# A complex recurrence and a mixture of experts on one core: less zero fill, a first slice in halves, spaced index casts, one more expert finished by rows

## Chip, cores and metric

The kernel runs on one core of one Trainium2 chip. The metric is the device time of one execution in microseconds. A measurement of this kernel can tell a difference of about 0.2% (1.3 us) from none.

## What is computed

The attention stage is a complex diagonal recurrence over 768 steps for 4 batches and 8 heads of 48 dimensions. Its output, 3072 rows of 384, goes through a router with one choice per row, eight experts of two layers (384 to 1024 to 384) and a capacity of 768 rows:

```python
mag = np.sqrt(a_re**2 + a_im**2)
scale = np.minimum(mag, 0.999) / (mag + 1e-06)
for t in range(S):
    S_re, S_im = ar*S_re - ai*S_im + outer(k[t], v[t]), ar*S_im + ai*S_re
    y[:, :, t] = np.einsum('bhd,bhde->bhe', q[:, :, t], S_re)
...
expert_idx = np.argmax(x @ w_gate, axis=1)
disp[e, counts[e]] = x[i]
h = np.maximum(disp @ w1, 0); y = h @ w2
out[i] = gate_w[i] * y[expert_idx[i], pos[i]]
```

## The kernel before, in words

**Attention.** The sequence is cut into 8 chunks of 96 positions, two chunks to a group `g` (0 to 3). For each group the decays are normalised in six slices of 8 rows (`norm`, L278: load of tile `a`, a square on ACT at L305, a sum of two squares, which PE does by identity matmuls into tile `n` at L272, then logarithm, exponent and corrections on ACT and DVE up to L374). `scan` multiplies the decays step by step on DVE (`xy` at L404, `a` at L409), `post` turns the products into weighted queries and keys (`qko`), which POOL writes to a DRAM scratch `scr`; SP reads them back as `qkc`. A `unit` (batch and chunk, 32 of them) transposes them (`tr`, L629), forms a masked product (`pa` L645, `a_sb` L649 on DVE), the state (`s_all` L660) and the output `y` (L706, L711), and writes the next chunk's state `z`, which POOL finishes by two accumulating DMAs (`z<-sx`, L673).

**Routing.** After the last unit of a cut (`CUTS`, pairs of group and unit count) `routing` picks the expert of each row: logits `lg` (L952) and counts `pp` (L970 to L975) on PE, choice, slot and place on DVE, then for each unit an index cast on DVE (`idx`, L1010) and an indirect DMA on POOL (`disp<-x,idx`, L1024) that scatters 96 rows into the experts' buffer `disp`, 448 rows of 386 words for each expert. Each such scatter is called a send below. `Plan.op(...).apart` keeps two sends apart in the plan, by `APART[b]` us.

**Fill.** Slots that no row reaches have to read as zero with an index out of bounds. Seven DMAs of 512 rows each, 772 KB (`disp<-fill`, L853), write all 3584 rows ahead of the first send.

**Experts.** `Moe.run` goes through 8 places of 8 steps. Place 0 is expert 0, the others are ordered by their counts, with 428 down to 372 rows (`WIDTH`). A step is 9 matmuls of the first layer (`ph`, L1220), ReLU split in two on ACT and DVE (`hh`, `hl`), and 9 of the second layer two steps later (`my`). Places 0 to 6 build the output with features on partitions (`second`, L1228), copy it to `ys` and turn it by PE (`yt`, L1174) before the scaling (`o`, L1184) and the scatter to the output. The last place has rows on partitions (`second_rows`, L1241) and needs neither copy nor turn.

**Order.** The order of attention and routing on every engine comes from `Plan.solve`: each step has an engine, a duration, a due time (`want`) and predecessors; a list scheduler fills the engines and the order is written out. On the chip every engine runs its list in that order and waits on semaphores alone; nothing holds a step back until its planned time. `BEGIN` holds the due times of the groups. `fill_gaps` puts warming matmuls of a 128x128 identity (`keep`, L226, in tile `s_all`) into planned idle time of PE of over 0.4 us that lies behind 82 us of the plan:

```python
if end > begin and gap > least:
    k = int((gap - .15) / one)
    out.append(Op("PE", 0, lambda k=k: keep(k), ...))
```

Of the kernel before, what the change touches and what calls it, by code (L numbers as in the profile page):

```python
# [180 lines left out]
class Att:  # L181
# [96 lines left out]
    def norm(self, g, j, s0):  # L278

# [27 lines left out]
        if g == 0 and j < 1:  # L307
            def xb():
                x = self.a4[g, j][:, 0:n, 3, :]
                nc.vector.tensor_tensor(out=x, in0=st['sq'][:, 0], in1=st['sq'][:, 1], op=ALU.add)  # L310
                st[0] = x
            o = plan.op(None, "DVE", dve(n * D), xb, w, after=[o], bufs=[a4_])
            parts = [(0, n, o, a4_)]
        elif by_dma:
# [66 lines left out]
    def scan(self, g, j, wants):  # L381
# [4 lines left out]
        a4_ = ("a4", g, j)  # L386
        for s in range(n - 1, -1, -1):
# [25 lines left out]
            m = plan.op(None, "DVE", .27, None, want, after=before + [K + ("i",), K + ("r",)], bufs=bufs)  # L413
# [316 lines left out]
    def routing(self, b, c, w, span):  # L730
# [55 lines left out]
CUTS = [(0, 8), (1, 8), (2, 8), (3, 5), (3, 6), (3, 7), (3, 8)]  # L786
# [4 lines left out]
class Route:  # L791
# [54 lines left out]
    def clear_ops(self):  # L846
# [190 lines left out]
class Moe:  # L1037
# [119 lines left out]
    def finish_ops(self, e, tail, py):  # L1157
# [35 lines left out]
    def run(self, order, perm, check):  # L1193
# [89 lines left out]
        for t in range(len(LAST)):  # L1283
# [150 lines left out]
def uncovered(nc, const, ps, sums, smalls, route, out):  # L1434


    bad = const.tile([128, NG + 2], F32, name="bad")
# [14 lines left out]
    nc.vector.tensor_reduce(out=bad[:C, NG + 1:NG + 2], in_=route.over, op=ALU.max, axis=AX.X)  # L1452
    one = const.tile([128, 1], F32, name="one")
# [12 lines left out]
def kernel(ctx, tc, q, k, v, a_re, a_im, w_gate, w1, w2, av, xv, cen, vp, out):  # L1466
# [5 lines left out]
    with ExitStack() as c_main, ExitStack() as c_att:  # L1472
# [143 lines left out]
```

## Time and profile before

| | |
|---|---|
| three runs | 640.61, 640.82, 641.45 us; median 640.82 |
| profiled execution, own time | 641.58 us |
| its span, first to last instruction | 639.9 us |
| mean granted TensorE clock | 0.936 of full |
| busy: PE, DVE, ACT, POOL | 561.8, 458.9, 383.5, 212.9 us |
| moved by DMA | 108.81 MB |

Times in the rows are microseconds from the start of the span. The kernel has two halves: attention and routing to 399 us, then the experts. Shares of the span are means over both; every statement below is read from one stage. A line number is that of the kernel before.

### The profile page before, as it was taken

Reading aid. Unit: us, or ns where it says so; the run is one execution under the profiler, and the core shown is the slowest. Engines: PE = TensorE matmul, PEld = TensorE weight load, DVE = VectorE, ACT = ScalarE, POOL = GpSimd, SP = SyncE. Lnnn points to the kernel's source line nnn. Section 1 sums busy time; section 2 is a strip of 40 time slices with the busy share of each in tenths; the row PEclk is TensorE's granted clock in tenths of the full one; section 3 lists DMA queues with packets and bytes.
Section 4 is the critical chain, followed back from the end, with each engine's and each line's share of the span. In section 5 each row is a group of like instructions: output and inputs, shape, how many; then the busy total and the mean of one; then the engine's idle time right before and its main releaser. Section 6 shows DMA issues by size and latency. Waiting matters only on the chain.

```text
span 639.9 us, 13273 instructions
## 1 busy us (share of the span) xinstructions
PE 561.8 (88%) x4662; PEld 489.7 (77%) x4662; DVE 458.9 (72%) x1340; ACT 383.5 (60%) x1034; POOL 212.9 (33%) x293
## 2 busy tenths in 40 slices
PE   2364569998999989999896889999999999999994
PEld 1122258786887868888785877999999999999993
DVE  3899979999999998999763244546665655655651
ACT  6465689989998899977652421344445344444540
POOL 9532314524459925464525031002020202112012
PEclk9666679999999999999999779999999999999997
DMA  6985588968899787885997231364545454455311
GB/s 214 297 245 147 147 203 231 241 189 207 196 230 251 213 228 168 213 223 135 215 242 209 55 91 29 109 184 125 163 129 158 138 169 155 155 165 159 101 37 37
DMA packets 75629, 108.81 MB, mean 170 GB/s; under 512 B 11716, under 2 KB 65853, under 8 KB 75553
## 3 DMA queue, kind: packets, MB, share of 16 engines
q1 hardware_dynamic: 58192, 57.37, 33.3%
q0 software_dynamic: 17360, 50.50, 29.1%
q8 instruction: 39, 0.64, 0.4%
q14 instruction: 38, 0.30, 0.2%
HBM read 71.51 MB, written 32.47 MB: 163 GB/s over the span
## 4 chain that ended last, share of the span: by engine, by line
PE 55%; DVE 20%; DMA 10%; ACT 9%; issue 4%; POOL 1%; POOLq 0%; DVEq 0%; ACTq 0%; SPq 0%
PE ph L1220 17%; PE my L1228 15%; DVE xy L404 4%; DMA scr<-qko 3%; DVE a L409 3%; PE pa L645 3%; PE tr L629 2%; DMA raw<-in_moe_w_dram 2%; PE n L272 2%; PE my L1241 2%; DMA qkc<-scr 2%; DVE qko L452 2%; PE s_all L660 2%; PE y L706 2%; DMA a<-in_av_dram 2%
## 5 line engine op out<-in xcount | busy, mean ns | idle before, releaser
L1266 ACT ACTIVATE hh<-ph 128x448 fp32r<-128x448 f32 (+7 forms) x64 | 32.7, 511 | 92.1 <-PE ph L1220 81.8
L1267 DVE SCALAR_TENSOR_TENSOR hl<-ph,hh 128x448 fp32r<-128x448 f32 (+7 forms) x64 | 37.2, 581 | 60.4 <-ACT hh L1266 59.6
L1185 POOL DMA_INDIRECT out_dram<-o,xr x26 | 25.7, 987 | 162.8 <-DVE o L1184 159.5
L1130 DVE TENSOR_TENSOR lo<-raw,hi 128x384 fp32r<-128x384 f32 (+2 forms) x128 | 65.7, 553 | 9.8 <-ACT hi L1129 9.7
L272 PE MATMUL n<-a,ident 128*128 128x384 f32 x92 | 44.8, 622 | 28.7 <-ACT a L305 28.7
L1220 PE MATMUL ph<-xh,hi 128*128 128x448 f32 (+7 forms) x192 | 69.5, 362 | 0.0
L1220 PE MATMUL ph<-xh,lo 128*128 128x448 f32 (+7 forms) x192 | 66.5, 347 | 0.0
L404 DVE TENSOR_TENSOR xy<-a 128x192 f32<-128x192 f32 (+1 forms) x199 | 61.5, 322 | 1.3 <-ACT a L374 1.1
L1129 ACT CAST hi<-raw 128x384 fp32r<-128x384 f32 (+2 forms) x128 | 59.1, 512 | 2.8 <-DMA raw<-in_moe_w_dram 2.8
L673 POOL DMA_DIRECT2D z<-sx x56 | 47.4, 1003 | 39.8 <-PE pa L645 12.4
L629 PE MATMUL tr<-ident,qkc 81*96 81x81 f32 x512 | 53.8, 241 | 5.6 <-DMA qkc<-scr 2.6
L1228 PE MATMUL my<-hh,lo 128*128 128x448 f32 (+6 forms) x168 | 58.7, 349 | 0.0
L1228 PE MATMUL my<-hh,hi 128*128 128x448 f32 (+6 forms) x168 | 58.6, 349 | 0.0
L1228 PE MATMUL my<-hl,hi 128*128 128x448 f32 (+6 forms) x168 | 58.6, 349 | 0.0
L649 DVE TENSOR_TENSOR a_sb<-pa,mask 96x384 f32<-96x384 f32 x64 | 35.1, 552 | 32.1 <-PE pa L645 21.1
L1024 POOL DMA_INDIRECT disp<-x,idx x32 | 42.1, 1315 | 46.1 <-DVE lm L961 22.4
L645 PE MATMUL pa<-qT,kT 128*96 128x96 f32 x512 | 56.9, 256 | 0.5 <-issue 0.4
L629 PEld LDWEIGHTS tr<-ident,qkc 81*96 81x96 f32 x512 | 43.3, 130 | 13.3 <-issue 4.0
L645 PEld LDWEIGHTS pa<-qT,kT 128*96 128x96 f32 x512 | 51.2, 170 | 2.5 <-issue 1.6
L272 PEld LDWEIGHTS n<-a,ident 128*128 128x128 f32 x92 | 20.0, 237 | 42.8 <-ACT a L305 24.6
L272 PE MATMUL p<-qko,ident 128*128 128x384 f32 x80 | 37.4, 598 | 15.3 <-ACT qko L441 15.2
L409 DVE TENSOR_TENSOR a<-xy 128x96 f32<-128x96 f32 (+1 forms) x218 | 49.8, 240 | 0.4
(224 smaller groups left out, 1459.0 us busy)
## 6 DMA issues: line engine op xcount, KB each, us to landing
raw<-in_moe_w_dram SPq DMA_DIRECT2D x64, 384.0 KB
qkc<-scr SPq DMA_DIRECT2D x32, 480.0 KB
scr<-qko POOLq DMA_DIRECT2D x44, 192.0 KB
scr<-qko POOLq DMA_DIRECT2D x20, 384.0 KB
a<-in_av_dram POOLq DMA_DIRECT2D x18, 384.0 KB
qkin<-in_xv_dram POOLq DMA_DIRECT2D x18, 384.0 KB
disp<-fill POOLq DMA_DIRECT2D x7, 772.0 KB
v<-in_vp_dram SPq DMA_DIRECT2D x32, 144.0 KB
```

The costliest lines, as they stand in the source:

```text
L272: nc.tensor.matmul(out=pt[:, :m], lhsT=self.ident, rhs=t[:, h:h + m], start=i == 0, stop=i == 1)
L404: nc.vector.tensor_tensor(out=st['xy'][:, :, cs].rearrange("p (u z) d -> p u z d", u=2), in0=a4[:, s, :, cs].rearrange("p (u z) d -> p u z ...
L409: nc.vector.tensor_tensor(out=self.a4[g, j][:, s, 0:2, cs], in0=xy[:, 0:4:2, cs], in1=xy[:, 1:4:2, cs], op=ALU.add)
L629: nc.tensor.transpose(out=pt[:, h * C:h * C + NE], in_=qk[:NE, 4 * hh + h, z_ * C:z_ * C + C], identity=self.ident[:NE, :NE])
L645: nc.tensor.matmul(out=pa[:, h * C:h * C + C], lhsT=kT[:, 4 * hh + h], rhs=qT[:, 4 * hh + h], start=True, stop=True)
L673: nc.gpsimd.dma_start(out=zn[a.start:a.stop or C], in_=st['sx'][o], accum_op=ALU.add)
L1024: ins = nc.gpsimd.indirect_dma_start(out=self.disp, out_offset=bass.IndirectOffsetOnAxis(ap=idx[:, c:c + 1], axis=0), in_=self.row(b, c0 + ...
L1129: return (lambda: nc.scalar.copy(out=hi[i][:, s], in_=raw[i][:, s]), lambda: nc.vector.tensor_tensor(out=lo[i][:, s], in0=raw[i][:, s], in ...
L1130: lambda: nc.vector.tensor_tensor(out=lo[i][:, s], in0=raw[i][:, s], in1=hi[i][:, s].bitcast(F32), op=ALU.subtract))
L1220: nc.tensor.matmul(out=ph[:, :W], lhsT=a[:, k, fs], rhs=r[:, k, :W], start=i == 0, stop=i == len(parts) - 1)
L1228: nc.tensor.matmul(out=py[m][:, :W], lhsT=a[:, f % self.PF, ms], rhs=r[:, :W], start=f == 0 and i == 0, stop=f == NF - 1 and i == 2)
L1267: nc.vector.scalar_tensor_tensor(out=hl[:, :W], in0=ph[:, :W], scalar=0.0, in1=hh[:, :W].bitcast(F32), op0=ALU.max, op1=ALU.subtract)
```

## The change

1. **Fill.** Place 0 is still filled whole (448 rows). Of the seven others only rows 320 to 447 are filled. `uncovered` adds a test: a smallest count under 320 sets the flag that sends the whole computation to the general path at the end. The fills are due at 9 and at 43 to 49 us of the plan, instead of 9, 12, 15 ... 27.
2. **First slice.** Slice (0, 0) goes through `norm_first` in two halves of four rows, the later rows first; the sum of squares stays on DVE. The scan of a row waits for its half alone. All five numbers of `BEGIN` are 3 lower.
3. **Casts.** `apart` is set on the cast (DVE), not on the send (POOL), with 5, 5, 2 and 1.4 us for the groups instead of 5, 5, 2.6 and 1. A new cut (3, 4) routes the first four units of the last group by themselves.
4. **Warming.** `fill_gaps` works from 58 us of the plan on instead of 82.
5. **Seventh place.** Places of three row tiles (`BY_ROWS`: places 6 and 7) use `second_rows`; place 6 loses its copies to `ys` and its turns.

```diff
     def norm(self, g, j, s0):
+        if g == 0 and j == 0:
+            self.norm_first(s0)
+        else:
+            self.norm_slice(g, j, s0)
+    def norm_first(self, s0):
...
+        for p, h in enumerate(range(n - HALF, -1, -HALF)):
+            i = slice(h, h + HALF)
...
+            o = plan.op(K + ("load", p), "SP", .6, load, v - 14, bufs=[a_], kb=48 * HALF, extra=2.)
+            o = plan.op(K + ("xa", p), "ACT", act(2 * m) + .1, xa, v, after=[o], bufs=[a_, a4_])
+            x_ = plan.op(None, "DVE", dve(m), xb, v, after=[o], bufs=[a4_])
...
+        def ready(s):
+            p = ((n - 1 - s) // HALF,) if g == 0 and j == 0 else ()
+            return [K + ("i",) + p, K + ("r",) + p]
...
             x = plan.op(None, "DVE", .12, fs['cast'][i], w + (5 + i) * s, after=[o])
-            o_ = plan.op(K(("send", i)), "POOL", 1.0, fs['send'][i], ...)
+            plan.op(K(("send", i)), "POOL", 1.0, fs['send'][i], ...)
             if rt.scattered is not None:
-                o_.apart = (rt.scattered, APART[b])
-            rt.scattered = o_
+                x.apart = (rt.scattered, APART[b])
+            rt.scattered = x
-BEGIN = (13, 67, 135, 203, 271)
+FILL = (9, 43, 44, 45, 46, 47, 48, 49)
+LEAST = 320
+HALF = 4
+BEGIN = (10, 64, 132, 200, 268)
-APART = (5, 5, 2.6, 1)
+APART = (5, 5, 2, 1.4)
-CUTS = [(0, 8), (1, 8), (2, 8), (3, 5), (3, 6), (3, 7), (3, 8)]
+BY_ROWS = [e for e, w in enumerate(WIDTH) if len(tiles(w)[1]) == KT]
+CUTS = [(0, 8), (1, 8), (2, 8), (3, 4), (3, 5), (3, 6), (3, 7), (3, 8)]
-        dv = self.disp.rearrange("(r p a) x -> r p a x", p=128, a=4)
-        return [lambda r=r: nc.gpsimd.dma_start(out=dv[r], in_=fill.unsqueeze(1).broadcast_to([128, 4, XW]))
-            for r in range(E_ * self.T // 512)]
+        dv = self.disp.rearrange("(e s) x -> e s x", e=E_)
+        def zero(e, s):
+            n = self.T - s
+            a = n // 16 if n < 256 else 4
+            p = n // a
+            nc.gpsimd.dma_start(out=dv[e, s:].rearrange("(p a) x -> p a x", a=a),
+                                in_=fill[:p].unsqueeze(1).broadcast_to([p, a, XW]))
+        return [lambda: zero(0, 0)] + [lambda e=e: zero(e, LEAST) for e in range(1, E_)]
-            pt = py[t] if e == E_ - 1 else turn(t)
+            pt = py[t] if e in BY_ROWS else turn(t)
-                if x[0] < E_ - 1:
-                    second(*x)
+                if x[0] in BY_ROWS:
+                    fin = self.finish_ops(x[0], rows[x[0]]['tail'], x[4]) if x[1] == NF - 1 else None
+                    for t in range(KT):
+                        second_rows(*x, t)
+                        if fin:
+                            fin[1 + t]()
+    nc.vector.tensor_scalar(out=bad[:C, NG + 2:NG + 3], in0=route.rank[:, E_ - 1:], scalar1=float(LEAST - T), scalar2=None, op0=ALU.is_lt)
-        plan.fill_gaps(att.keep)
+        plan.fill_gaps(att.keep, begin=58.)
```

How the order moves, at three places. First POOL near the start, where constants end and the first stores of `scr` begin. Before, with the last two of seven fills there:

```order
L874 TENSOR_TENSOR key<-key,dec 96x8
L877 MEMSET room 96x1 x8
L853 DMA disp<-fill 512x1x386 x2
L498 DMA scr_1_97<-qko_0_327 64x8x96
L495 DMA scr_1_97<-qko_0_327 64x1536
L498 DMA scr_1_97<-qko_0_327 64x8x96
L498 DMA scr_1_97<-qko_1_391 64x8x96
L293 DMA a_0_460<-in_av_dram 128x2x384
```

and now:

```order
L972 TENSOR_TENSOR key<-key,dec 96x8
L975 MEMSET room 96x1 x8
L586 DMA scr_1_97<-qko_0_331 64x8x96
L583 DMA scr_1_97<-qko_0_331 64x1536
L586 DMA scr_1_97<-qko_0_331 64x8x96
L586 DMA scr_1_97<-qko_1_404 64x8x96
L384 DMA a_0_469<-in_av_dram 128x2x384
L583 DMA scr_1_97<-qko_1_404 64x1536
L586 DMA scr_1_97<-qko_1_404 64x8x96
L950 DMA disp<-fill 128x1x386 x2
L586 DMA scr_1_97<-qko_2_471 64x8x96
L950 DMA disp<-fill 128x1x386
```

One fill of 448 rows stays ahead of this piece; the seven small ones stand between the stores of slices 1 to 3 of group 0.

Second, PE from the start to the end of group 0 (`n` are sums of a slice's decays, `ptok` the token numbers that a mask on DVE needs, `pt` and `te` the turns at the group's end). Before, the rows up to `ptok` and those around `pt`:

```order
L272 MATMUL n_1_0_174<-a_0_1_168,ident 128x384 x2
L272 MATMUL n_2_0_190<-a_0_2_182,ident 128x384 x2
L272 MATMUL n_3_0_254<-a_0_3_248,ident 128x384 x2
L240 MATMUL ptok<-ident,tokrow 96x96
```

```order
L272 MATMUL n_1_0_607<-a_1_1_599,ident 128x384 x2
L272 MATMUL p_4_0_624<-qko_4_605,ident 128x384 x2
L563 MATMUL pt_684<-ident,pend_678 96x128 x2
L272 MATMUL n_2_0_708<-a_1_2_696,ident 128x384 x2
L521 MATMUL te_1_0_716<-ident,qko_5_673 96x128 x4
L521 MATMUL te_1_4_727<-ident,qko_5_673 96x128 x4
```

and now:

```order
L272 MATMUL n_1_0_190<-a_0_1_180,ident 128x384 x2
L272 MATMUL n_2_0_218<-a_0_2_204,ident 128x384 x2
L240 MATMUL ptok<-ident,tokrow 96x96
L272 MATMUL p_0_0_339<-qko_0_331,ident 128x384 x2
L272 MATMUL n_3_0_354<-a_0_3_336,ident 128x384 x2
```

```order
L272 MATMUL p_4_0_622<-qko_4_616,ident 128x384 x2
L272 MATMUL n_1_0_646<-a_1_1_626,ident 128x384 x2
L226 MATMUL s_all<-ident 128x128 x18
L272 MATMUL n_2_0_723<-a_1_2_698,ident 128x384 x2
L651 MATMUL pt_740<-ident,pend_695 96x128 x2
L609 MATMUL te_1_0_744<-ident,qko_5_690 96x128 x4
```

`ptok` no longer stands behind the sum of slice 3, and 18 warming matmuls stand ahead of the sum of slice 2 of group 1, itself now ahead of `pt`.

Third, DVE at the end of the routing of group 2 (`a_sb` are the masked products of the next units). Before, eight casts in two bunches:

```order
L1006 TENSOR_REDUCE fine<-ok_0_4836 96x1
L1010 CAST idx_0_4844<-slot_0_4803 96x1 x3
L649 TENSOR_TENSOR a_sb_123<-pa_6_0_4815,mask 96x384
L649 TENSOR_TENSOR a_sb_123<-pa_6_1_4852,mask 96x384
L1010 CAST idx_0_4844<-slot_0_4803 96x1 x5
L649 TENSOR_TENSOR a_sb_122<-pa_7_0_4920,mask 96x384
```

and now, the first five of eight:

```order
L1104 TENSOR_REDUCE fine<-ok_0_4891 96x1
L1108 CAST idx_0_4899<-slot_0_4858 96x1
L737 TENSOR_TENSOR a_sb_123<-pa_6_0_4870,mask 96x384
L737 TENSOR_TENSOR a_sb_123<-pa_6_1_4907,mask 96x384
L1108 CAST idx_0_4899<-slot_0_4858 96x1 x2
L737 TENSOR_TENSOR a_sb_122<-pa_7_0_4968,mask 96x384
L1108 CAST idx_0_4899<-slot_0_4858 96x1
L737 TENSOR_TENSOR a_sb_122<-pa_7_1_4994,mask 96x384
L1058 TENSOR_REDUCE mx_0_5036<-lg_0_5016 96x4
L1059 TENSOR_TENSOR lm_0_5037<-lg_0_5016,mx_0_5036 96x32
```

The casts now alternate with masked products that wait for PE, and with the choice of the new cut.

## Rows read from the trace of the kernel before

**Rows 1.** The page, part 2: PE's granted clock in 40 slices.

```profile
PEclk9666679999999999999999779999999999999997
```

**Rows 2.** Busy time by stretch: PE, PEld, DVE, ACT, POOL, clock, DMA share, GB/s.

```profile
30.00:40.00 10.00, 5.49 (x8) 2.52 (x8) 10.00 (x35) 5.06 (x10) 2.68 (x4) 0.54 1.03 336
...
100.00:120.00 20.00, 19.84 (x211) 15.73 (x210) 20.00 (x55) 19.39 (x63) 11.18 (x16) 1.00 0.93 234
...
400.00:640.00 240.00, 230.69 (x1310) 224.27 (x1309) 133.06 (x283) 99.11 (x219) 29.43 (x30) 0.99 0.44 132
```

**Rows 3.** The chain that ended last, first 20 us: start, duration, what.

```profile
0.82 3.81 DMA a<-in_av_dram
...
12.01 6.04 DMA a<-in_av_dram
```

**Rows 4.** Timeline, DVE, first 25 us: start, duration, engine, line; idle before and releaser.

```profile
13.04 0.43 DVE L404 TENSOR_TENSOR xy<-a 128x96 f32<-128x96 f32 x2 [1.12 <-ACT a L374]
...
13.63 0.55 DVE L344 TENSOR_TENSOR lnn<-n,lnn 128x384 f32<-128x384 f32 x1
...
14.10 0.35 DVE L404 TENSOR_TENSOR xy<-a 128x192 f32<-128x192 f32 x1
...
22.38 0.25 DVE L242 TENSOR_TENSOR mask<-ptok,tokrow 96x96 f32<-96x96 f32 x1 [2.33 <-ACT tokcol L241]
```

**Rows 5.** The same chain: sums of slices near the end of group 0, and one later.

```profile
74.45 2.93 PE n L272 x4
...
85.62 2.93 PE n L272 x4
...
127.64 1.35 PE n L272 x4
```

**Rows 6.** Busy time by stretch, columns of rows 2, group 0 into group 1.

```profile
86.00:90.00 4.00, 4.00 (x13) 2.50 (x13) 3.90 (x15) 2.13 (x6) 1.42 (x2) 0.50 1.08 244
```

**Rows 7.** Timeline, POOL, first and last send of two bursts.

```profile
342.19 1.04 POOL L1024 DMA_INDIRECT disp<-x,idx  x1 [0.30 <-DVE a_sb L649]
...
350.93 0.92 POOL L1024 DMA_INDIRECT disp<-x,idx  x1 [0.30 <-issue]
370.44 0.93 POOL L1024 DMA_INDIRECT disp<-x,idx  x1 [18.58 <-DVE lm L961]
...
375.38 0.92 POOL L1024 DMA_INDIRECT disp<-x,idx  x1 [0.30 <-ACT qT L633]
```

**Rows 8.** Timeline, PE and ACT, stops inside the bursts.

```profile
352.12 0.55 PE L924 MATMUL y<-xt,wg 128*32 128x96 f32 x8 [5.37 <-issue]
...
374.76 0.26 PE L711 MATMUL y<-qT,z 128*48 128x96 f32 x1 [0.49 <-issue]
...
377.65 0.29 PE L629 MATMUL tr<-ident,qkc 81*96 81x81 f32 x1 [1.14 <-issue]
...
351.58 0.48 ACT L900 COPY xt<-y 128x384 f32<-128x384 f32 x1 [8.34 <-remote]
```

**Rows 9.** Busy time by stretch, columns of rows 2, behind the stops.

```profile
352.00:360.00 8.00, 6.39 (x60) 5.82 (x60) 1.11 (x2) 2.78 (x9) 0.00 (x0) 0.50 0.36 89
...
377.60:384.00 6.40, 6.35 (x47) 5.64 (x48) 1.81 (x7) 1.69 (x5) 0.37 (x1) 0.51 0.41 111
```

**Rows 10.** A lone send of group 1, and the stretch that holds four such.

```profile
264.28 1.01 POOL L1024 DMA_INDIRECT disp<-x,idx  x1 [3.20 <-DVE idx L1010]
...
260.00:280.00 20.00, 19.87 (x236) 16.77 (x236) 19.73 (x69) 17.64 (x53) 9.98 (x13) 1.00 0.77 196
```

**Rows 11.** Timeline, PE: eleven warming matmuls, two passes each.

```profile
386.67 2.70 PE L226 MATMUL s_all<-ident 128*128 128x128 f32 x22
```

**Rows 12.** Timeline, PE: six of place 6's turns, and the matmul behind them.

```profile
610.78 0.82 PE L1174 MATMUL yt<-ident,ys 128*128 128x128 f32 x6
611.36 0.42 PE L1220 MATMUL ph<-xh,hi 128*128 128x372 f32 x1
```

**Rows 13.** Timeline, POOL: the longest send of group 0.

```profile
205.72 5.92 POOL L1024 DMA_INDIRECT disp<-x,idx  x1 [0.30 <-issue]
```

More of the change, by code (lines that the diff above doesn't have):

```diff
@@ L280, in norm, with norm_slice @@
+    def norm_slice(self, g, j, s0):
         nc, plan = self.nc, self.plan
@@ L306, in norm @@
         o = plan.op(K + ("xa",), "ACT", act(2 * n * D) + .1, xa, w, after=[K + ("load",)], bufs=[a_, a4_])
[L307 to L314, printed above, removed]
+        if by_dma:
             def acc():
@@ L412, in scan @@
             before = [("s", g) + prev[1:]] if ("s", g) + prev[1:] in plan.names else []
-            m = plan.op(None, "DVE", .27, None, want, after=before + [K + ("i",), K + ("r",)], bufs=bufs)
+            m = plan.op(None, "DVE", .27, None, want, after=before + ready(s), bufs=bufs)
             a = plan.op(("s", g, j, s), "DVE", .169, None, want, after=[m], bufs=[a4_, xy_])
@@ L750, in routing @@
             x = plan.op(None, "DVE", .12, fs['cast'][i], w + (5 + i) * s, after=[o])
-            o_ = plan.op(K(("send", i)), "POOL", 1.0, fs['send'][i], w + (5 + i) * s, after=[x] + ([("mload",)] if (b, c + 1) in LATE else []), kb=148, extra=2.)
+            plan.op(K(("send", i)), "POOL", 1.0, fs['send'][i], w + (5 + i) * s, after=[x] + ([("mload",)] if (b, c + 1) in LATE else []), kb=148, extra=2.)
             if rt.scattered is not None:
-                o_.apart = (rt.scattered, APART[b])
-            rt.scattered = o_
+                x.apart = (rt.scattered, APART[b])
+            rt.scattered = x
 RINGS = dict(qkc=3, v=3, qT=2, kT=2, a_sb=2, z=5, s_sb=4, sx=4, xt=2, tr=2, pa=2, s=1, ad=2, y=1,
@@ L1238, in second_rows @@
             hi, lo = (w[1] for w in self.w[e, f // self.PF])
-            ts, m = slice(t * LP, t * LP + LAST[t]), LAST[t]
+            P, parts = tiles(WIDTH[e])
+            m = parts[t]
+            ts = slice(t * P, t * P + m)
             for i, (a, r) in enumerate(((hh, hi), (hl, hi), (hh, lo))):
@@ L1269, in run @@
             if f == 0:
-                py[e] = [self.ps.tile([128, 512], F32, tag=f"y{m}", name=f"my{m}_{e}") for m in range(len(LAST) if e == E_ - 1 else KT)]
+                py[e] = [self.ps.tile([128, 512], F32, tag=f"y{m}", name=f"my{m}_{e}") for m in range(KT)]
             queue.append((e, f, hh, hl, py[e]))
@@ L1273, in run @@
                 x = queue.pop(0)
-                if x[0] < E_ - 1:
+                if x[0] in BY_ROWS:
[4 more added lines that the diff above has]
+                            fin[1 + t]()
+                else:
                     second(*x)
-                else:
-                    for t in range(len(LAST)):
-                        second_rows(*x, t)
             for op in later.pop(s, []):
@@ L1282, in run @@
         fin = self.finish_ops(e, rows[e]['tail'], py[e])
-        for t in range(len(LAST)):
+        for t in range(KT):
             for x in queue:
@@ L1434, in uncovered @@
 def uncovered(nc, const, ps, sums, smalls, route, out):
-    bad = const.tile([128, NG + 2], F32, name="bad")
+    bad = const.tile([128, NG + 3], F32, name="bad")
     nc.vector.memset(bad, 0.0)
@@ L1456, in uncovered @@
     pb = ps.tile([128, 512], F32, tag="tr", name="pbad", bufs=2)
-    nc.tensor.matmul(out=pb[0:1, :NG + 2], lhsT=one, rhs=bad, start=True, stop=True)
+    nc.tensor.matmul(out=pb[0:1, :NG + 3], lhsT=one, rhs=bad, start=True, stop=True)
     flag = const.tile([1, 1], F32, name="flagf")
-    nc.vector.tensor_reduce(out=flag, in_=pb[0:1, :NG + 2], op=ALU.add, axis=AX.X)
+    nc.vector.tensor_reduce(out=flag, in_=pb[0:1, :NG + 3], op=ALU.add, axis=AX.X)
     nc.vector.tensor_scalar(out=flag, in0=flag, scalar1=1.0, scalar2=None, op0=ALU.min)
@@ L1492 @@
         moe_plan(plan, box, early)
-        for r in range(E_ * T // 512):
-            plan.op(("fill", r), "POOL", .9, lambda r=r: box['fill'][r](), 9 + 3 * r, kb=772)
+        for r in range(E_):
+            plan.op(("fill", r), "POOL", .9, lambda r=r: box['fill'][r](), FILL[r], kb=1.55 * (T - (LEAST if r else 0)))
         order = plan.solve()
-        plan.fill_gaps(att.keep)
+        plan.fill_gaps(att.keep, begin=58.)
         cut = max(i for i, o in enumerate(order) if o.idx < early) + 1
```

63 lines of the change are left out of this document (62 added, 1 removed).

## The prediction

> **What bounds the kernel now.** I read the page's clock line first, because it splits the span without any theory. In slices of 16 us, PE's granted clock is at 6 or 7 from 16 to 96 us, at 7 in the two slices from 352 to 384 us and in the last, and at 9 elsewhere [rows 1]. Then I read busy time by stretch. Near the start DVE is full (10.00 of 10 us) while PE works eight matmuls in ten microseconds [rows 2]: there the scan on DVE sets the pace. At 100 to 120 us PE, DVE and ACT are all full (19.84, 20.00 and 19.39 of 20), so no single saving counts there, only a lead brought in from earlier. The experts, from 400 us, are PE alone: 230.69 of 240 us busy [rows 2]; what PE need not do there is won one for one.
>
> Next the chain that ended last, for what lies ahead of each stage. A slice's load starts at 0.82 and takes 3.81 us, a later one takes 6.04 [rows 3]. The DVE timeline shows the scan's first step at 13.04, and a mask that waits 2.33 us for a token column from ACT [rows 4]. Near 74 to 90 us the chain runs through sums on PE that take 2.93 us, where the same sum later takes 1.35 [rows 5]; the clock in that stretch is 0.50, PE's lower level, 1.2 GHz instead of 2.4 [rows 6].
>
> Last the end of attention. Two bursts of sends, eight in 342.19 to 351.85 and five in 370.44 to 376.30 [rows 7], enclose gaps on PE that no data explains: 5.37 us, later 0.49 and 1.14 with "issue" as releaser, while ACT waits 8.34 us for "remote" [rows 8]. Behind each gap PE works at half clock for some 8 and 6 us and is then nearly full (6.39 of 8, 6.35 of 6.4), DVE almost empty (1.11 of 8) [rows 9]. A difference of 0.2%, about 1.3 us, is the least that a measurement of this kernel can tell.
>
> **The change part by part.** The sum is made against the profiled execution's own time, 641.58 us (span 639.9 and 1.7 around it); the median of the three runs, 640.82, is 0.76 lower.
>
> *A, the start.* The first slice's load lands at 0.82 + 3.81 = 4.63 [rows 3], the first step starts at 13.04 [rows 4]: 8.4 us of links over 384 columns. On DVE 384 columns take 0.55 us and 192 take 0.35 [rows 4], a factor of 0.64. If all links shrink so, the first step starts 8.4 x 0.36 = 3.0 us earlier. Against it, seven DVE operations become fourteen: 7 x (2 x 0.35 - 0.55) = 1.05, on the engine that sets the pace. Net 2.0. The mask's 2.33 goes too: its token column needs `ptok` on PE, which stood behind the sum of slice 3, whose load took 6.04 us beside the fills [rows 3]. Now `ptok` stands ahead of that sum, and early fills drop from seven times 0.79 MB to one of 0.69, with 1.38 MB more at 43 to 49 us of the plan. Sum A = 4.3; bounds 0 (DVE is delayed again by ACT's extra instructions, the lead goes) and 3.0 + 2.3 = 5.3.
>
> *B, warming from 58 us.* Two sums at 2.93 instead of 1.35 lie on the chain [rows 5], 3.2 us; the rest of that stretch is PE full and DVE at 3.90 of 4 [rows 6], where a faster PE frees little. The price: 18 warming matmuls in a row ahead of the sum of slice 2. Eleven took 2.70 us [rows 11], so 18 take 4.4 at full clock and twice that at half. They are planned into idle time; if PE is not idle on the chip when they come, they delay a sum. Bounds: +3.7 (both sums and a small rest) and -3. I take 3.0, since the two sums are themselves the rows at half clock.
>
> *C, the end of attention.* What the bursts cost: the gap of 5.37, the trickle gaps 0.49 + 1.14 with the like on other passes, some 2.6 together [rows 8], and half clock behind them, (6.39 + 6.35) / 2 = 6.4 [rows 9]. Together 14.4. Evidence that sends cause it: PE stops about three microseconds after a burst begins and starts again as it ends, twice; a lone send does nothing, since four of them stand in a stretch where PE has 19.87 of 20 us and clock 1.00 [rows 10]. In the bursts sends follow each other by (350.93 - 342.19) / 7 = 1.25 and (375.38 - 370.44) / 4 = 1.24 us [rows 7]; now casts release them, planned 2 us apart in group 2 and 1.4 in group 3, in turn with masked products. Bounds 0 and 14.4. I take 11: nearer the upper end, because group 2, with the larger loss, is spread most, but two of its casts still stand together, and 1.4 is close to 1.24. The extra cut (3, 4) adds some 19 small DVE operations, each below the 0.35 of a 192-column one [rows 4], at most 6.6 us; they are hidden where DVE is idle (1.11 of 8 busy [rows 9]), and would be paid if that cover went. A send now stands on POOL behind a cast that stands behind a masked product, and behind the send wait `z` and `scr`; that is the rival below.
>
> *D, place 6 by rows.* Its nine turns go. Six take 611.36 - 610.78 = 0.58 us of PE's time [rows 12], nine 0.9. Their overlapping durations, 0.82 for six, give the upper bound 1.2; the lower is 0, if `second_rows` waits for ReLU more often. The copies to `ys` are on ACT and DVE, which are under 0.6 busy in that half [rows 2]: nothing.
>
> *At nothing:* the test on the smallest count, hidden beside the experts on DVE [rows 2]. On these inputs the reference's router gives each expert 338 to 421 rows, the smallest over 320, so the general path is not taken.
>
> Sum: 4.3 + 3.0 + 11 + 0.9 = 19.2. 641.58 - 19.2 = 622.4, at the median's level 621.6; I say **621.5**.
>
> **The rivals.**
>
> *R1: spacing does not end the stops.* The stops might come from something that falls with the bursts (the scattered rows on their way, 1.4 us apart or not), and the gap and the half clock stay. For it: the releaser is "issue", not a send [rows 8], and 1.4 is near 1.24. Against it: two bursts, two stops, no stop at lone sends [rows 10]. Then A + B + D = 8.2 remain: 640.8 - 8.2 = 632.6.
> The Trainium skill, page "SBUF — State Buffer", section "Who interferes with whom", says that only DVE and GpSimd (POOL here) contend, for one shared pair of ports, and "PE and ACT never wait on anyone"; by it sends could not stop PE, C would be 0, and the time would be R1's. The trace speaks against that so far: PE and ACT both stop inside a burst [rows 8].
>
> *R2: the lead of A and B is lost before the experts.* A group's scan runs against its due times and all three engines are full at 100 to 120 us [rows 2]; a lead can go into a wait for a load or a store. For it: slices wait for DMAs of 6.04 us [rows 3] whose start the fills no longer delay but whose bandwidth (336 GB/s at 30 to 40 us [rows 2]) they share at 43 to 49 us now. Against it: the order is a chain without fixed times. Then C + D = 11.9: 628.9.
>
> *R3, slower: POOL is held by sends.* Each of the 24 sends of groups 0 to 2 waits at POOL's head for a cast that DVE reaches only after masked products; `z` behind it comes late, so does the next unit's output on PE, which delays the masked product again. POOL waited 3.20 us for such a cast [rows 10] and a send once held it 5.92 us [rows 13]. It decides from 19.2 / 24 = 0.8 us of delay per send on; at 1.0 us the time is 640.8 - 19.2 + 24 = 645.6. Against it: the wait of 3.20 stood in a stretch in which PE lost nothing [rows 10].
>
> *R4: no change*, the gains of A to C each fall to their lower bounds: 640.
>
> **How the numbers follow.** Forecast 0.57; R1 0.20 (two bursts are little evidence, and the pace changes little in group 3); R2 0.12 (each group hands its lead on through one list); R3 0.07; R4 0.04, the general path included, far below 0.01. The forecast's own range: upper bounds give 5.3 + 3.7 + 14.4 + 1.2 = 24.6, so 616.2, and 615 with the 0.8 between runs; on the other side, C at 5 and B at 1 instead of 11 and 3 give 629.5. The range must take in R2 (628.9) and R1 (632.6), and R1 with A halved and B at 1.5, 636.2: **615 to 636**, which leaves out R3, R4 and a little of R1. Faster by over 0.2%: 0.57 + 0.20 + 0.12 = 0.89. Same 0.04. Slower 0.07.
>
> **What the changed profile would show.** A right: the first scan step at about 10 us, no wait ahead of the mask. B right: sums near 75 to 90 us at about 1.35 and clock near 1 there; wrong, if the 18 warming matmuls are followed by a late sum or the clock stays at 0.50. C right: the clock line without a 7 between 350 and 384 us, sends 1.4 us apart or more, no PE gap of over 1 us by "issue"; R1, if the gap and the half clock are there at a slower pace. D right: no `yt` in place 6, and the stretch from the first expert matmul to the end shorter by 0.9. R2: the scan of group 1 starts 7 us earlier, the experts hardly. R3: POOL's sends idle behind `idx` for microseconds in groups 0 and 1, `z` behind them, and PE below 19 of 20 us at 260 to 280. The prediction is wrong if the time is above 636, and its main step is wrong if the clock line keeps its dips.

## The result, and the profile after

The changed kernel takes 623.18 us (median of 4 runs, 622.16 to 626.55) against 640.98 before (4 runs on the same chip, 640.61 to 641.45): ratio 0.9731, interval 0.9693 to 0.9769, 17.8 us less. The prediction said 621.5 in 615 to 636. The sum was right; two of its terms were not, and one of its premises holds on some chips only. Medians below take in every run; the ratios leave out two slow ones, 643.6 us of burst_tail_3 and 719.07 us of the kernel before on chip 1.

The profiled execution took 622.75 us, its span is 621.0. The page's clock line answers to [rows 1]:

```profile
PEclk9676999999899999999989999999999999999998
```

The two 7s at 352 to 384 us are gone. Busy time by stretch (PE, PEld, DVE, ACT, POOL, clock, DMA share, GB/s) answers to [rows 2, 6, 9, 10]:

```profile
30.00:40.00 10.00, 4.69 (x9) 2.38 (x9) 10.00 (x38) 5.51 (x11) 1.53 (x3) 0.67 0.51 135
86.00:90.00 4.00, 3.87 (x57) 3.40 (x56) 3.86 (x16) 3.43 (x11) 1.02 (x2) 1.00 0.92 236
100.00:120.00 20.00, 19.02 (x197) 15.34 (x196) 19.67 (x60) 19.72 (x61) 9.82 (x14) 1.00 0.97 229
260.00:280.00 20.00, 19.57 (x222) 15.97 (x222) 19.96 (x60) 18.73 (x57) 12.90 (x16) 1.00 0.81 218
341.00:344.00 3.00, 2.19 (x32) 1.75 (x26) 0.26 (x1) 0.42 (x2) 1.29 (x2) 1.00 1.03 312
352.00:360.00 8.00, 7.16 (x99) 6.42 (x97) 4.63 (x26) 3.26 (x12) 3.67 (x4) 1.00 0.32 95
```

At 86 to 90 us and at 352 to 360 us the clock is 1.00 instead of 0.50. DVE is nearly as full at 30 to 40 and 100 to 120 us as it was. The DVE timeline answers to [rows 4]: first scan step and mask.

```profile
9.54 0.36 DVE L492 TENSOR_TENSOR xy<-a 128x192 f32<-128x192 f32 x1 [0.23 <-ACT a L353]
...
16.60 0.25 DVE L242 TENSOR_TENSOR mask<-ptok,tokrow 96x96 f32<-96x96 f32 x1 [0.79 <-ACT tokcol L241]
```

The POOL timeline, first four sends of group 2, answers to [rows 7]: three still follow each other by 1.3 us, less than the 1.4 that the prediction named as its sign; the fourth comes after 3.5.

```profile
339.07 1.03 POOL L1122 DMA_INDIRECT disp<-x,idx  x1 [0.75 <-DVE idx L1108]
340.41 0.96 POOL L1122 DMA_INDIRECT disp<-x,idx  x1 [0.30 <-issue]
341.68 0.92 POOL L1122 DMA_INDIRECT disp<-x,idx  x1 [0.30 <-issue]
345.14 0.92 POOL L1122 DMA_INDIRECT disp<-x,idx  x1 [2.54 <-ACT lt L1025]
```

Where the time came from is read best by the first transposes of units 0, 8, 24 and 28 and the first matmul of the experts, on the PE timeline. Before:

```profile
88.35 0.88 PE L629 MATMUL tr<-ident,qkc 81*96 81x81 f32 x5
...
157.25 0.46 PE L629 MATMUL tr<-ident,qkc 81*96 81x81 f32 x4 [1.14 <-DMA qkc<-scr]
...
310.95 0.48 PE L629 MATMUL tr<-ident,qkc 81*96 81x81 f32 x4
...
341.74 0.45 PE L629 MATMUL tr<-ident,qkc 81*96 81x81 f32 x4
...
399.14 0.45 PE L1220 MATMUL ph<-xh,hi 128*128 128x448 f32 x1
```

and after:

```profile
79.65 0.52 PE L717 MATMUL tr<-ident,qkc 81*96 81x81 f32 x5
...
153.21 0.48 PE L717 MATMUL tr<-ident,qkc 81*96 81x81 f32 x4 [0.68 <-ACT ends L615]
...
307.94 0.46 PE L717 MATMUL tr<-ident,qkc 81*96 81x81 f32 x4 [1.58 <-DMA qkc<-scr]
...
339.13 0.58 PE L717 MATMUL tr<-ident,qkc 81*96 81x81 f32 x6
...
381.50 0.45 PE L1318 MATMUL ph<-xh,hi 128*128 128x448 f32 x1
```

The lead is 8.7 us at the first unit, 4.0 at group 1's, 3.0 at group 3's, 2.6 at that group's fifth, then 17.6 at the experts, and 18.9 at the end of the span (639.9 - 621.0). So in this pair of traces the end of attention gives 17.6 - 2.6 = 15.0 us, everything ahead of it 2.6. The 2.6 is known roughly only: runs scatter ahead of this place. The kernel before starts its fifth unit of the last group at 341.74 here and at 346.02 in a second trace (before_again, below); the changed kernel starts it at 339.13 and 339.07, and d_undone, which differs from it in the experts alone, at 342.31. The stretch behind it scatters less: from the fifth unit to the experts, five traces (after_again, a_undone, b_undone, d_undone, fill_undone) lie between 39.3 and 39.4 us.

### The profile page after: what moved, and what is told of

It reads as the page before. It is cut to its first block, busy times and chain, and to the rows that moved or that the text cites. A ratio compares the mean times of both kernels' runs of the same rounds, so it can differ in the third digit from the quotient of the medians.

```text
span 621.0 us, 13432 instructions
## 1 busy us (share of the span) xinstructions
PE 558.5 (90%) x4705; PEld 489.3 (79%) x4705; DVE 462.1 (74%) x1370; ACT 384.2 (62%) x1043; POOL 203.9 (33%) x294
## 4 chain that ended last, share of the span: by engine, by line
PE 56%; DVE 17%; ACT 16%; DMA 4%; POOL 3%; issue 2%; POOLq 0%; ACTq 0%; SPq 0%; DVEq 0%
PE ph L1318 17%; PE my L1326 13%; PE my L1341 4%; DVE xy L492 3%; PE pa L733 3%; ACT z L768 3%; PE tr L717 3%; DVE a L497 2%; PE s_all L748 2%; PE y L794 2%; DVE qko L575 2%; DMA scr<-qko 2%; DMA a<-in_av_dram 2%; PE y L799 1%; PE yt L1272 1%
## 5 line engine op out<-in xcount | busy, mean ns | idle before, releaser
L272 PE MATMUL n<-a,ident 128*128 128x384 f32 x92 | 41.8, 586 | 20.1 <-ACT a L396 20.0
L272 PE MATMUL p<-qko,ident 128*128 128x384 f32 x80 | 36.0, 580 | 16.2 <-ACT qko L529 16.2
L1326 PE MATMUL my<-hl,hi 128*128 128x448 f32 (+5 forms) x144 | 50.6, 351 | 0.0
L1326 PE MATMUL my<-hh,lo 128*128 128x448 f32 (+5 forms) x144 | 50.6, 351 | 0.0
L1326 PE MATMUL my<-hh,hi 128*128 128x448 f32 (+5 forms) x144 | 50.5, 351 | 0.0
L1122 POOL DMA_INDIRECT disp<-x,idx x32 | 35.7, 1114 | 41.0 <-ACT lt L1025 9.7
L1318 PE MATMUL ph<-xl,hi 128*128 128x448 f32 (+7 forms) x192 | 45.8, 347 | 0.0
```

Source lines behind the costliest of these rows:

```text
L272: nc.tensor.matmul(out=pt[:, :m], lhsT=self.ident, rhs=t[:, h:h + m], start=i == 0, stop=i == 1)
L1122: ins = nc.gpsimd.indirect_dma_start(out=self.disp, out_offset=bass.IndirectOffsetOnAxis(ap=idx[:, c:c + 1], axis=0), in_=self.row(b, c0 + ...
L1318: nc.tensor.matmul(out=ph[:, :W], lhsT=a[:, k, fs], rhs=r[:, k, :W], start=i == 0, stop=i == len(parts) - 1)
L1326: nc.tensor.matmul(out=py[m][:, :W], lhsT=a[:, f % self.PF, ms], rhs=r[:, :W], start=f == 0 and i == 0, stop=f == NF - 1 and i == 2)
```

## The experiments

Every kernel ran beside the kernel before on the same chip, but not all on one chip. The difference between chips turned out to be the main finding, so the table gives the kernel before on each chip. "Ratio" is to that kernel, with its interval. The intervals reach 0.2 to 0.9% each way, so a single part worth 1 or 2 us is often not resolved by the times alone.

| run | chip | kernel before, us | this, us | ratio |
|---|---|---|---|---|
| the change, first comparison | not recorded | 640.98 | 623.18 | 0.9731 (0.9693 to 0.9769) |
| burst_tail | 3 | 625.32 | 617.42 | 0.9884 (0.9847 to 0.9921) |
| c_undone | 3 | 625.32 | 619.88 | 0.9933 (0.9902 to 0.9964) |
| a_undone | 3 | 625.32 | 618.66 | 0.9895 (0.9867 to 0.9923) |
| b_undone | 3 | 625.32 | 620.28 | 0.9924 (0.9900 to 0.9948) |
| before_again | 1 | 626.50 | 625.25 | 0.9995 (0.9969 to 1.002) |
| after_again | 1 | 626.50 | 619.75 | 0.9910 (0.9877 to 0.9943) |
| d_undone | 1 | 626.50 | 620.54 | 0.9915 (0.9885 to 0.9945) |
| fill_undone | 1 | 626.50 | 619.72 | 0.9898 (0.9862 to 0.9935) |
| burst_tail_2 | 0 | 626.03 | 619.00 | 0.9896 (0.9842 to 0.9949) |
| cd_only | 9 | 640.23 | 625.91 | 0.9783 (0.9743 to 0.9823) |
| burst_tail_3 | 7 | 639.22 | 632.50 | 0.9869 (0.9781 to 0.9957) |
| wider_pace | 7 | 639.80 | 624.65 | 0.9747 (0.9715 to 0.9779) |

### The pace of the sends taken back: burst_tail

```diff
-APART = (5, 5, 2, 1.4)
+APART = (5, 5, 0, 0)
```

> The changed kernel with the casts of groups 2 and 3 not kept apart (APART 5, 5, 0, 0): POOL's list is the same row for row, on DVE three and then five casts of group 2 stand together, and four of the first cut of group 3. Theory (bursts stop PE): the stop and the half clock come back in the stretch from 339 us on, the experts start 10 to 15 us later than at 381.5, time 633 to 638 us. Rival (what was won there comes from the extra cut, the warming or another order, not from the pace): no stop, 622 to 625 us.

Measured 617.42 us, below both. There is no stop (PE works 7.94 of 8 us from 341.8 us on, clock 1.00), but the kernel before itself took 625 on that chip, not 641, so this run decides neither for the theory nor for the rival.

### The whole third part taken back: c_undone

```diff
-            plan.op(K(("send", i)), "POOL", 1.0, ...)
+            o_ = plan.op(K(("send", i)), "POOL", 1.0, ...)
             if rt.scattered is not None:
-                x.apart = (rt.scattered, APART[b])
-            rt.scattered = x
+                o_.apart = (rt.scattered, APART[b])
+            rt.scattered = o_
-APART = (5, 5, 2, 1.4)
+APART = (5, 5, 2.6, 1)
-CUTS = [(0, 8), (1, 8), (2, 8), (3, 4), (3, 5), (3, 6), (3, 7), (3, 8)]
+CUTS = [(0, 8), (1, 8), (2, 8), (3, 5), (3, 6), (3, 7), (3, 8)]
```

> The changed kernel with the whole third part taken back: apart on the send, 5, 5, 2.6 and 1, no cut (3, 4). The prediction's size of this part, 11 us: 634 us. The reading of the two traces (a lead of 2.6 us when the last group's fifth unit starts, 17.6 when the experts start, so 15.0 from the end of attention): 638 us. If both parts of it count, this is slower than burst_tail; if the pace is all, it is the same.

Measured 619.88 us; the changed kernel itself came to 619.75 on another chip of this kind. Both sizes were too high, by 14 and 18 us: on such a chip the times show no worth of this part. In the traces, the stretch from the last group's fifth unit to the experts is 40.2 us here and 39.3 in the changed kernel, so it is worth some 0.9 there.

### The early parts taken back: a_undone, b_undone, fill_undone

a_undone sends the first slice through the code for whole slices (with its sum of squares on DVE) and sets `BEGIN` 3 higher:

```diff
-        if g == 0 and j == 0:
-            self.norm_first(s0)
-        else:
-            self.norm_slice(g, j, s0)
+        self.norm_slice(g, j, s0)
...
-BEGIN = (10, 64, 132, 200, 268)
+BEGIN = (13, 67, 135, 203, 271)
```

> The changed kernel with the first slice whole again and BEGIN 3 higher; the small fills stay. The prediction's size, about 2.0 for the slice (the mask's 2.3 goes with the fill and stays won): 625 us. The rival R2 (the lead is lost before the experts): 623 us. By the trace the last scan ends 4.8 us earlier than before and the fifth unit of the last group starts 2.6 earlier: 625 to 627 us.

Measured 618.66 us, less than any of the three: without the halves the kernel is not slower. In its trace the first unit starts 5 us later than in the changed kernel (84.47 against 79.65), but the last group's fifth unit starts earlier (336.22 against 339.13).

```diff
-        plan.fill_gaps(att.keep, begin=58.)
+        plan.fill_gaps(att.keep)
```

> The changed kernel with warming from 82 us of the plan on again. The prediction's size: 3.0 us, so 626 us, with the first unit's transposes some 3 to 4 us later than at 79.7. By the trace of the changed kernel (first unit 8.6 us ahead, group 1's first unit only 4.0): the lead of this part goes in the stretch where DVE is full, and the time stays at 622 to 624 us, while the first unit still starts later.

Measured 620.28 us, 0.5 more than the changed kernel on a chip of this kind, which is within both intervals. Its first unit does not start later either, as both cases expected, but at 77.74 us against 79.65. The chain of waits of b_undone has the two slow sums back, behind a slice's load (start, duration, what):

```profile
61.03 8.10 DMA a<-in_av_dram
...
70.14 2.93 PE n L272 x4
...
81.20 2.93 PE n L272 x4
```

and its busy time by stretch the lower clock, 0.57 at 80 to 86 us; from 86 us on it is 1.00, as in the changed kernel:

```profile
80.00:86.00 6.00, 4.80 (x21) 3.43 (x22) 4.98 (x16) 4.22 (x12) 0.93 (x2) 0.57 0.56 175
86.00:90.00 4.00, 4.00 (x45) 3.25 (x44) 3.18 (x12) 3.94 (x12) 0.48 (x1) 1.00 0.82 223
```

In the changed kernel the chain of waits has no such sum there, but the same load, and behind it almost only pieces of ACT and DVE of under 2 us each up to 94 us. Its load, and its busy time at 80 to 86 us:

```profile
61.13 9.37 DMA a<-in_av_dram
...
80.00:86.00 6.00, 4.66 (x34) 3.33 (x32) 5.84 (x19) 5.73 (x15) 0.40 (x1) 1.00 0.70 209
```

So the sums go from the chain, and work of ACT and DVE in the same stretch (5.73 and 5.84 of 6 us) takes their place; the chain of the kernel before had no load there, and the scan that starts earlier now meets one.

fill_undone fills all eight experts whole, at the old times:

```diff
-FILL = (9, 43, 44, 45, 46, 47, 48, 49)
+FILL = (9, 12, 15, 18, 21, 24, 27, 30)
-        ... [lambda e=e: zero(e, LEAST) for e in range(1, E_)]
+        ... [lambda e=e: zero(e, 0) for e in range(1, E_)]
```

> The changed kernel with all eight experts filled whole, at 9 to 30 us of the plan. The prediction's size: the mask's 2.3 us more than after_again, seen as a later scan of group 0. Rival (DVE finds other work, or the mask is not what sets the scan): the same within 0.2%.

Measured 619.72 us: the rival, no difference. The mask's wait is back (2.41 us against 0.83 in after_again), but it does not set the first unit: that starts at 79.96 us, against 79.65 and 79.22 in the changed kernel's two traces.

### The two kernels themselves on another chip: before_again, after_again

> The kernel before itself, for a trace on this chip: in the first four comparisons it took 625.3 us (17 runs), not 641. Theory (the stops of PE inside the two bursts are not there on this chip): no PE gap of over 1 us by issue at 345 to 378 us, clock near 1 there, experts at about 384 instead of 399. Rival (the stops are there and the time is won elsewhere): the gap of 5 us again, and an earlier first unit.

> The changed kernel itself, on this chip. If all but the end of attention is worth what the first two traces show (2.6 us at the last group's fifth unit, 1.05 in the experts, 0.25 behind them): 621 us against 625. If the changed kernel is as slow here as where it was first measured, 623 us; then c_undone (619.9) says that the third part costs 3 us where there are no stops.

before_again took 625.25 us, after_again 619.75. The busy time of before_again behind its first sends of group 2 (346.46 on) shows PE full at full clock, where [rows 8, 9] had a stop and half clock:

```profile
346.00:352.00 6.00, 6.00 (x91) 5.51 (x89) 1.95 (x9) 3.25 (x10) 4.48 (x6) 1.00 1.03 280
352.00:360.00 8.00, 8.00 (x129) 7.29 (x127) 2.31 (x8) 4.52 (x15) 3.21 (x4) 1.00 0.60 182
```

Its sends come at the same pace:

```profile
346.46 1.04 POOL L1024 DMA_INDIRECT disp<-x,idx  x1 [0.30 <-DVE a_sb L649]
...
355.20 0.92 POOL L1024 DMA_INDIRECT disp<-x,idx  x1 [0.30 <-ACT qT L621]
```

(355.20 - 346.46) / 7 = 1.25 us. So the same program with the same burst stops on one chip and not on another. From the last group's fifth unit to the experts, before_again

```profile
346.02 0.72 PE L629 MATMUL tr<-ident,qkc 81*96 81x81 f32 x8
...
387.26 0.45 PE L1220 MATMUL ph<-xh,hi 128*128 128x448 f32 x1
```

takes 387.26 - 346.02 = 41.2 us, where the first trace of this kernel takes 399.14 - 341.74 = 57.4. The changed kernel tells the same on a small scale. Of after_again, its fifth unit, busy time and the ACT row where the three sends stand together:

```profile
339.07 0.72 PE L717 MATMUL tr<-ident,qkc 81*96 81x81 f32 x8
...
341.00:344.00 3.00, 3.00 (x47) 2.63 (x42) 0.61 (x2) 1.76 (x6) 1.24 (x2) 1.00 1.07 320
...
341.63 0.48 ACT L998 COPY xt<-y 128x384 f32<-128x384 f32 x1 [1.27 <-PE y L799]
```

and the same ACT row of the first trace of the changed kernel:

```profile
343.58 0.48 ACT L998 COPY xt<-y 128x384 f32<-128x384 f32 x1 [3.16 <-PE pa L733]
```

PE 3.00 of 3.00 us against 2.19, ACT's wait 1.27 against 3.16: where the kernel before stops for 5.4 us in eight sends, the changed kernel stops briefly in three. It starts its experts at 378.37 on chip 1 and at 381.50 in the first trace, from fifth units that start at the same time (339.1): 39.3 us against 42.4.

### The seventh place by turns again: d_undone

```diff
-BY_ROWS = [e for e, w in enumerate(WIDTH) if len(tiles(w)[1]) == KT]
+BY_ROWS = [E_ - 1]
```

> The changed kernel with place 6 finished by turns again. The prediction's size: 0.9 us more than after_again (bounds 0 and 1.2), all of it between the first expert matmul and the last.

Measured 620.54 us against 619.75, inside the scatter of runs. The trace resolves it: first and last start of the experts' first matmul and last layer (a line's own summary: min/median/max ns, first and last start). after_again:

```profile
L1318 PE MATMUL ph<-xh,hi x192: 328/349/453, 378.4 to 603.0; 128*128 128x448 f32 x24, 128*128 128x428 f32 x24, 128*128 128x412 f32 x24, 128*128 128x408 f32 x24
...
L1341 PE MATMUL my<-lo,hh x48: 332/336/339, 561.5 to 608.5; 128*128 128x384 f32 x40, 128*116 128x384 f32 x8
```

d_undone:

```profile
L1318 PE MATMUL ph<-xh,hi x192: 328/349/453, 381.7 to 607.3; 128*128 128x448 f32 x24, 128*128 128x428 f32 x24, 128*128 128x412 f32 x24, 128*128 128x408 f32 x24
...
L1341 PE MATMUL my<-lo,hh x24: 332/336/338, 592.1 to 612.9; 128*128 128x384 f32 x16, 128*116 128x384 f32 x8
```

612.9 - 381.7 = 231.2 against 608.5 - 378.4 = 230.1: the part is worth 1.1 us.

### Looking for a chip with stops: burst_tail_2, cd_only, burst_tail_3

> burst_tail once more, for another chip. On both chips so far the kernel before took 625 us and PE did not stop inside its bursts; where it took 641, it did. If this run's kernel before takes 641 again: theory (closely spaced sends set the stops off there) says that burst_tail takes 633 us or more, with PE gaps by issue near 343 to 350; the rival (something else in the kernel before sets them off) says 620 to 624. If the kernel before takes 625: 617 to 620, no stops.

The kernel before took 626.03 on this chip, and burst_tail_2 619.00. Its busy time by stretch and its first and last send of group 2:

```profile
343.00:351.00 8.00, 7.94 (x112) 7.11 (x110) 3.88 (x21) 4.69 (x16) 4.91 (x6) 1.00 0.88 279
351.00:359.00 8.00, 7.97 (x113) 7.28 (x110) 4.66 (x28) 4.24 (x14) 4.59 (x5) 1.00 0.32 93
...
339.80 1.03 POOL L1122 DMA_INDIRECT disp<-x,idx  x1 [0.75 <-DVE idx L1108]
...
348.51 0.92 POOL L1122 DMA_INDIRECT disp<-x,idx  x1 [0.30 <-ACT xt L998]
```

cd_only is the changed kernel with a_undone, b_undone and fill_undone in one: of the change, parts 3 and 5 stay.

> The kernel before with the third and fifth parts alone: whole first slice, BEGIN, large early fills and warming from 82 as before. Where the kernel before takes 625 us: if the lead of the early parts is what the change is worth there (its scan ends 4.8 us earlier, place 6 is worth 1.05), 624 us; if the parts stand in for one another (each taken back alone cost at most 1.4), 620 us. Where it takes 641: theory (the spaced sends shorten the stops, 12 of the 17.8 us) 627 us, PE gaps of at most 1.5 us at 340 to 378; rival (they do not) 638 or more.

Here the kernel before took 640.23. cd_only took 625.91: 14.3 us less, 1.1 of them place 6 (by d_undone), so some 13.2 are the third part's. Its busy time by stretch keeps small losses (PE 5.10 of 6, 6.85 of 8), but the clock is full:

```profile
340.00:346.00 6.00, 5.10 (x76) 4.43 (x75) 2.24 (x13) 2.33 (x8) 2.90 (x3) 1.00 0.68 181
...
352.00:360.00 8.00, 6.85 (x92) 6.25 (x90) 4.54 (x31) 2.63 (x9) 4.22 (x5) 1.00 0.27 77
```

> burst_tail a third time, for a chip like the last one, on which the kernel before took 640.2 and cd_only 625.9. There: theory (the pace of the sends is what shortens the stops) 633 us or more, with PE gaps of over 3 us in all at 340 to 352; rival (the extra cut and the order of the masked products do it, not the pace) 621 to 625. On a chip where the kernel before takes 625: 617 to 620, as twice before.

The kernel before took 639.22, burst_tail_3 632.50 (four runs, 628.5 to 643.6). Busy time, sends, ACT, PE and the start of the experts, to be laid beside burst_tail_2:

```profile
343.00:351.00 8.00, 1.66 (x11) 1.24 (x11) 0.00 (x0) 0.01 (x1) 4.61 (x6) 0.63 0.49 157
351.00:359.00 8.00, 7.48 (x67) 6.73 (x67) 2.04 (x7) 2.91 (x10) 0.00 (x0) 0.51 0.35 86
...
339.51 1.03 POOL L1122 DMA_INDIRECT disp<-x,idx  x1 [0.76 <-DVE idx L1108]
...
348.22 0.92 POOL L1122 DMA_INDIRECT disp<-x,idx  x1 [0.30 <-issue]
...
350.99 0.48 ACT L998 COPY xt<-y 128x384 f32<-128x384 f32 x1 [10.14 <-remote]
351.52 0.55 PE L1022 MATMUL y<-xt,wg 128*32 128x96 f32 x8 [5.70 <-ACT xt L998]
...
391.33 0.45 PE L1318 MATMUL ph<-xh,hi 128*128 128x448 f32 x1
```

One program, the same eight sends 1.24 us apart: in 343 to 351 us PE works 7.94 of 8 us on chip 0 and 1.66 on chip 7, DVE 3.88 and 0.00, ACT 4.69 and 0.01, and only POOL goes on (4.91, 4.61). On chip 7 PE runs at half clock behind it (0.51), on chip 0 at full. ACT stops ahead of PE: it waits 10.14 us up to 350.99, and PE, which works on until 345.8, then waits 5.70 us for ACT's copy `xt`. The experts start at 391.3 us; with the spaced casts, in the first trace, at 381.5, from fifth units at 339.55 and 339.13. This is the theory's case: on a chip with stops, the bunched sends bring them back, for some 9 us (632.5 - 623.2, on two chips; the interval of 632.5 is wide, 0.9% each way).

### Wider spacing: wider_pace

```diff
-APART = (5, 5, 2, 1.4)
+APART = (5, 5, 2.5, 2)
```

> The changed kernel with APART 5, 5, 2.5, 2: no two casts of groups 2 and 3 stand together any more on DVE. Where the kernel before takes 640 us: if closeness of sends is the cause, what was left of the stops in the changed kernel (3.1 us between the fifth unit of the last group and the experts, against the same kernel on a chip without stops) goes: 620 to 621 us against 623. If each send has its own price there, whatever the distance, 623 to 625. Where the kernel before takes 625: there is nothing to win, and sends that come later hold the last experts' rows back, 620 to 623.

Measured 624.65 us beside 639.80, ratio 0.9747, not better than the change (0.9731). It is on the same chip as burst_tail_3 and differs from it in the pace alone: 632.50 against 624.65, nearly 8 us for the pace. Busy time by stretch:

```profile
340.00:350.00 10.00, 10.00 (x153) 9.08 (x151) 3.97 (x20) 5.21 (x17) 3.80 (x4) 1.00 0.92 242
350.00:360.00 10.00, 9.42 (x129) 8.56 (x128) 5.53 (x34) 4.60 (x15) 4.58 (x5) 1.00 0.23 68
360.00:370.00 10.00, 8.96 (x124) 7.70 (x120) 7.01 (x46) 3.44 (x12) 3.67 (x4) 1.00 0.24 67
```

Ahead of 350 us PE loses nothing any more: what was left of the stop is gone, as the first case expected, though the time is that of the second. After that it loses 0.6 and 1.0 us in ten, in waits for ACT and DVE, and the last sends come later (380.1 instead of 377.9), the experts at 385.4. So spacing has a price too, and going beyond 2 and 1.4 us won nothing; other spacings were not tried. No version measured here beats the change on chips with stops; on the others burst_tail and a_undone lie 2 and 1 us lower, in overlapping intervals.

## Why the prediction was right, and where it was not

**The sum** was 19.2 us; the two spans differ by 18.9. By the traces it is made up of 2.6 (A and B), 15.0 (the stretch of C), 1.1 (D) and 0.2 behind the last matmul, where the prediction had 7.3, 11 and 0.9. A and B came out 4.7 lower and C 4.0 higher; that these errors cancel was luck, and so was the chip: beside a kernel before of 626.50 us, on chip 1, the same change gave 6.75 us.

**C, mis-sized by 4.** The mechanism held. The size is seen when the stretch from the last group's fifth unit to the experts is laid side by side with and without stops: 57.4 and 41.2 us in the kernel before, 42.4 and 39.3 in the changed one. The stops cost 57.4 - 41.2 = 16.2 us, where the prediction read 14.4 from the gaps and the half clock; 42.4 - 39.3 = 3.1 of it was left, where the discount to 11 left 3.4. So the discount, for the pair of casts and the pace near 1.24, was about right. The other 41.2 - 39.3 = 1.9 us are won without any stop, and the prediction had them at nothing; 0.9 of them are the third part's by c_undone (40.2), the rest is not explained. All but the 39.3 rests on one trace each, and the chips differ; cd_only gives 13.2 for the part by times. The pace is the larger share, nearly 8 us by the two kernels on chip 7 and 51.8 - 42.4 = 9.4 by the stretch of burst_tail_3. What the extra cut (3, 4) does to a stop no run here separates. Without stops, burst_tail and burst_tail_2, which have the cut and no spacing, take 38.5 and 38.9 us for the stretch: there the cut gains a little and the spacing costs a little.

**A, right at its place and lost later.** The first step came at 9.54, 3.5 us earlier (forecast: about 10), the mask's wait fell from 2.33 to 0.79. The prediction let this lead run to the end; a_undone and fill_undone show no loss when either is taken back. What failed is the step from "DVE sets the pace near the start" to "4.3 us at the end": the halves are worth 5 us at the first unit and nothing measurable at the end. Group 3's first unit waits 1.58 us for `qkc<-scr` after the change, where before it waited for nothing (the transposes at 310.95 and 307.94 above), and a load of 9.37 us stands on the chain at 61 us: a lead that turns into waits for DMAs, which is R2's mechanism.

**B, right about the clock, wrong about the price.** The warming lifts the clock at 80 to 86 us, from 0.57 in b_undone to 1.00, and takes the two sums of 2.93 us from the chain. The rise at 86 to 90 us, shown above, is no proof of it, because b_undone has 1.00 there too. Without the early warming the kernel took only 0.5 us more by the times (620.28 - 619.75, on two chips), not 3.0, and its first unit started no later: DVE and ACT are at 5.84 and 5.73 of 6 us at 80 to 86 after the change, so they end last in the sums' place. A piece of the chain that ended last is worth only its distance to the next chain. Together A and B with the fill are worth 2.6 by the traces, and 625.91 - 623.18 = 2.7 by cd_only (on two chips).

**What single parts do not add up to.** Of the 6.75 us on chip 1, 1.9 lie in the stretch before the experts and 1.1 in the experts; the rest, some 3.7, must lie ahead of it. No part of A, B or the fill, taken back alone, loses as much: 618.66, 620.28 and 619.72 us against 619.75. They may stand in for one another. No run without stops had two of them taken back, so which of them gives it is not shown.

**D**, 1.1 for 0.9, inside its bounds of 0 to 1.2.

**The rivals.** R1 (632.6): fallen on the chips with stops, where the clock dips went and burst_tail_3 brought the first back. On chips without stops spacing ends no stop, because there is none, and the change is worth 0.9% (0.991, interval 0.9877 to 0.9943). The Trainium skill, page "SBUF — State Buffer", section "Who interferes with whom", would have PE and ACT wait on no other engine; it speaks of ports, and burst_tail_3 shows PE at 1.66 and ACT at 0.01 of 8 us while POOL works on. Since burst_tail_2, the same program, has no stop, ports that are the same on both chips do not explain the difference. R2 (628.9): its mechanism was there, 6 of the first 8.7 us were lost before the last group's fifth unit, but C made up for them. R3 (slower): POOL's sends do wait for their casts (2.54 us ahead of the fourth, above; the row names an ACT step, but the send's cast runs on DVE only at 344.21), but PE keeps 19.57 of 20 us at 260 to 280, with four sends, so the price stays far under the 0.8 us per send from which it would decide.

**The premise.** "Evidence that sends cause it: twice, and not at lone sends" was right in the main for one trace from one chip, with two slips. The stretch of 260 to 280 us holds three sends before the change and not four (264.28, 269.48, 275.50; the next is at 280.10). And the gap of 5.37 us on PE is not one "that no data explains": the matmul behind it, at 352.12, reads the copy `xt` that ACT wrote from 351.58 to 352.06 [rows 8], and the same gap in burst_tail_3 names ACT. What no data explains is ACT's wait of 8.34, and the short gaps on PE ahead of it. One trace could not show that the stop belongs to that chip as much as to the burst.

## What to carry to other kernels

A stop of all engines with "issue" or "remote" as releaser may depend on the chip: run the same program on several before its cost is taken for the kernel's own, and compare only runs of one chip. Before such a gap is put down to its own engine, look at what the next instruction there reads. Here spacing indirect DMAs cost little and kept such stops short; too much of it puts the last send late. A lead at the start is worth what is left of it where the next stage waits, so read it at several places on the way.

## What was not expected of the hardware

The kernel before takes 625 to 626.5 us on chips 0, 1 and 3 and 639 to 641 on chips 7 and 9 and in the first comparison. Nearly all of the difference lies in one place, the stretch from the last group's fifth unit to the experts (57.4 us against 41.2): with eight indirect DMAs about 1.24 us apart, ACT and DVE stop for 8 to 11 us and PE, behind them, for 5 to 6 on the one kind and not at all on the other, and PE's clock is at its lower level for some 8 us behind it. The loss was larger with more sends in a row: PE lost 0.8 of 3 us in three sends, 6.3 of 8 in eight. What in the chip, or beside it at that time, makes the difference stays open; no run here looked at it. Only chip 7 was met twice, with stops both times. The share of the extra cut and the third part taken back whole on a chip with stops were not tried.
